# ScalarE issues the loads into buffer A from the first V block on, SyncE those into buffer B

## The chip, the core and the metric

The kernel runs on one core of a Trainium2 chip. The metric is the device time of the program in microseconds (us), the median of several executions. A profiled execution of the same program gives the trace that is quoted below: its times are counted from the first instruction of the span.

Five engines work side by side, each through its own list of instructions: TensorE (PE in the profile, with its weight loads as PEld), VectorE (DVE), ScalarE (ACT), GpSimd (POOL) and SyncE (SP). They wait for each other on semaphores. Loads from the device memory (HBM) are done by 16 DMA engines; a load is issued by an instruction in the list of one of these engines. In the profile, queue q1 holds what SyncE issued and q10 what ScalarE issued.

## What is computed

One decode step of a transformer layer for two sequences: grouped-query attention over a cache of 32768 positions with 32 query heads and 4 KV heads of width 128, in parallel with a SiLU feed-forward block, both on the layer-normed input and both added to it. Everything is float32.

```python
# x: (2, 1, 1024)
xn = layernorm(x)
q = (xn @ wq).reshape(B, 1, 32, 128)                     # wq: (1024, 4096)
k, v = repeat(k_cache, 8), repeat(v_cache, 8)            # caches: (2, 4, 32768, 128)
p = softmax(einsum("bhqd,bhkd->bhqk", q, k) * 128**-0.5)
o = einsum("bhqk,bhkd->bhqd", p, v)
attn = o.reshape(B, 1, 4096) @ wo                        # wo: (4096, 1024)
ffn = silu(xn @ w1) @ w2                                 # w1: (1024, 3584), w2: (3584, 1024)
return x + attn + ffn
```

With one token per sequence nearly all of the data is used once: the caches alone are 268 MB, and 331.4 MB are read in all.

## The kernel before, in words

**Two large buffers.** SBUF holds two buffers, `bufA` and `bufB` (`buf[0]` and `buf[1]`), of 64 KB in each of the 128 partitions, 8.4 MB each. Everything that is read in bulk passes through them in a fixed sequence of 40 steps, alternately A and B: `wq` in two halves, `w1` in two parts, then for each of the 8 pairs of KV head and sequence (`it` in the code) the steps K0 (A), K1 (B), V0 (A), V1 (B), and at the end `wo` in two halves, the first part of `w2` (`w2a`, A, in two pieces) and the second (`w2b`, B, in seven pieces). A full load is one DMA instruction of 128 rows of 64 KB; the 16 DMA engines take 8 rows each.

**TensorE** works through the steps in this order: it waits for the landing of the step's load (`taken`, through `ld`) and for the small operand (`tok`), then runs 64 matmuls of 128x512 over the buffer (`slots`) into PSUM (`xy`), and marks the step as done on `turn_sem`. The buffer is then free.

**VectorE** stands between: with `relay(n)` it waits for the mark of a step and adds one to the semaphore `freed`, on which the loads wait. In `attend()` it relays K0 and K1, then works out the softmax up to the subtraction of the maximum (a transpose, a reduction, two small matmuls on TensorE in between, a subtraction), raises `subbed`, relays V0 and V1, reduces the result, and raises `normed`.

**ScalarE** has a loop of its own over `it`: it waits for `subbed`, does two exponentials that write the weights for V0 and V1 (and raise `tok`), waits for `normed`, and copies the result away (which lets GpSimd stage the weights of the next K0 and K1 through `stage()`).

**SyncE** issues the loads. `load(k, dst, src, s, n)` waits for the event that frees the buffer (`step(n)`: from step 3 on, `freed` has reached n - 2, which means that the step two before, in the same buffer, is done) and issues the DMA. All loads from `w1` to `w2b` stand in SyncE's one list, in the order of the steps. ScalarE issues one DMA, the small `x` (32 KB) at the start.

A step here is named by its block and the value of `it`: K1 of it 0 is the second K block of the first pair.

Of the kernel before, what the change touches and what calls it, by code (L numbers as in the profile page):

```python
# [8 lines left out]
B, HQ, HKV, SK, DH, D, F = 2, 32, 4, 32768, 128, 1024, 3584  # L9
P = 128  # L10
REP = HQ // HKV
W = 16384
# [6 lines left out]
STEPS = 4 + 4 * LOOPS + 4  # L19
# [32 lines left out]
def gqa_plus_mlp_kernel(nc, x8, kt, v0, v1, wq, wo, w1a, w1b, w2a, w2b, out):  # L52
# [4 lines left out]
    sp, T, V, A, G = nc.sync, nc.tensor, nc.vector, nc.scalar, nc.gpsimd  # L57
    sems = [pe.sem, dve.sem, act.sem, pool.sem]

    def sem(name):  # L60
        sems.append(nc.alloc_semaphore(name))
        return sems[-1]

    def sb(name, *shape):
        return nc.alloc_sbuf_tensor(name, shape, F32).ap()
# [4 lines left out]
    buf = [sb(n, P, W) for n in ("bufA", "bufB")]  # L70
    ld, more, tok = ([sem(f"{n}{k}") for k in "AB"] for n in ("ld", "more", "tok"))
# [89 lines left out]
    def step(n):  # L161
        return (turn_sem, n) if n <= 2 else (freed, n - 2)

    def load(k, dst, src, s, n):
        if n:
            sp.wait_ge(*step(n))
        sp.dma_start(buf[k][:, dst] if isinstance(dst, slice) else dst, src).then_inc(s, 16)  # L167

    every = slice(0, W)
    load(0, buf[0].rearrange("p (a n) -> p a n", a=2)[:, :, :6144], w1b, ld[0], 1)  # L170
    load(1, every, w1a, ld[1], 2)
    for it in range(LOOPS):
        h, b = divmod(it, B)
        for j, src in enumerate((kt[b, h, 0], kt[b, h, 1], v0[b, h], v1[b, h])):
            load(j % 2, every, src, ld[j % 2], 3 + 4 * it + j)
    load(0, every, wo[0], ld[0], STEPS - 5)
    load(1, every, wo[1], ld[1], STEPS - 4)
    load(0, slice(0, W // 2), w2a[:, :W // 2], ld[0], STEPS - 3)
    load(0, slice(W // 2, W), w2a[:, W // 2:], more[0], 0)
    cuts = [0, 6 * D, 8 * D, 9 * D, 10 * D, 11 * D, 11 * D + 4 * CUT, 12 * D]  # L180
    for lo, hi, s in zip(cuts, cuts[1:], [ld[1], more[1], *last]):
        load(1, slice(lo, hi), w2b[:, lo:hi], s, STEPS - 2 if lo == 0 else 0)
# [2 lines left out]
    for n in range(4):  # L185
# [6 lines left out]
        a, b = ev[n][:, :512], ev[n][:, 512:]  # L192
# [37 lines left out]
           tqs[:, :, ::16].rearrange("p (h m) b -> p h b m", m=REP)).then_inc(tq, 1)  # L230
    for it in range(LOOPS):
        h, b = divmod(it, B)
        act.wait((subbed, it + 1))
        for c in range(NC):
            A.activation(wt[c].rearrange("p e m -> p (e m)"), st[:, 1024 * c:1024 * c + 1024], AF.Exp,  # L235
                         scale=SCALE).then_inc(tok[c], 1)
        act.wait((normed, it + 1))
        A.copy(oT[:, REP * h:REP * (h + 1), 16 * b], onew).then_inc(tq, 1)  # L238
    for s in (trm, tgd):
        A.sem_inc(s, 1)  # L240
    outs = []
    for n in range(3):
        act.wait(step(STEPS - 3 + n) if n < 2 else (turn_sem, 5))
# [205 lines left out]
```

## Time and profile before

| what | us |
|---|---|
| median of 3 runs | 772.49 (772.41 to 772.53) |
| span of the profiled execution | 771.0 |
| TensorE busy, matmuls | 389.6 |
| VectorE busy | 132.3 |
| GpSimd busy | 44.2 |
| ScalarE busy | 28.4 |

The span is the time from the first to the last instruction of the one profiled execution; the device time of the runs holds a little more, so the median stands 1.5 us above the span. In a row of the timeline the first number is the start, the second the duration, then engine, line, operation and the tiles; what stands in brackets is how long the engine was idle before it, and for whom it waited. "SPq" and "ACTq" are the DMA-issuing instructions of SyncE and ScalarE: the duration there is that of issuing, not of the transfer.

### The profile page before, as it was taken

Reading aid. Unit: us, or ns where it says so; the run is one execution under the profiler, and the core shown is the slowest. Engines: PE = TensorE matmul, PEld = TensorE weight load, DVE = VectorE, ACT = ScalarE, POOL = GpSimd, SP = SyncE. Lnnn points to the kernel's source line nnn. Section 1 sums busy time; section 2 is a strip of 40 time slices with the busy share of each in tenths; the row PEclk is TensorE's granted clock in tenths of the full one; section 3 lists DMA queues with packets and bytes.
Section 4 is the critical chain, followed back from the end, with each engine's and each line's share of the span. In section 5 each row is a group of like instructions: output and inputs, shape, how many; then the busy total and the mean of one; then the engine's idle time right before and its main releaser. Section 6 shows DMA issues by size and latency. Waiting matters only on the chain. (4 is left out here: it accounts for less than half of the span.)

```text
span 771.0 us, 6110 instructions
## 1 busy us (share of the span) xinstructions
PE 389.6 (51%) x2702; PEld 124.5 (16%) x2702; DVE 132.3 (17%) x98; ACT 28.4 (4%) x37; POOL 44.2 (6%) x65
## 2 busy tenths in 40 slices
PE   0454545455545454645455545444645455545466
PEld 0111211121112111211121112111211121112122
DVE  2000104030403040304030303040303030313000
ACT  0000100100010001000100010001000100010000
POOL 3001200000000100010001000100010001000121
PEclk9967677776677777677776677777677776677688
DMA  9999999999999999999999999999999999999997
GB/s 383 435 435 435 435 435 435 435 435 435 435 435 435 435 435 435 435 435 435 435 435 435 435 428 428 418 428 432 425 432 435 435 435 435 435 435 435 435 432 331
DMA packets 6944, 331.40 MB, mean 430 GB/s; under 512 B 776, under 2 KB 920, under 8 KB 1440
## 3 DMA queue, kind: packets, MB, share of 16 engines
q1 hardware_dynamic: 6928, 331.37, 99.5%
q10 hardware_dynamic: 16, 0.03, 0.0%
HBM read 331.38 MB, written 0.02 MB: 430 GB/s over the span
## 5 line engine op out<-in xcount | busy, mean ns | idle before, releaser
L107 PE MATMUL xy<-bufB,weights 128*32 128x512 f32 x1248 | 176.2, 727 | 169.3 <-PEq L49 169.3
L107 PE MATMUL xy<-bufA,weights 128*32 128x512 f32 x1280 | 180.4, 726 | 101.0 <-PEq L49 101.0
L107 PEld LDWEIGHTS xy<-bufB,weights 128*32 128x32 f32 x1248 | 48.8, 131 | 296.7 <-issue 296.5
L107 PEld LDWEIGHTS xy<-bufA,weights 128*32 128x32 f32 x1280 | 49.6, 130 | 215.5 <-issue 215.5
L258 DVE STREAM_TRANSPOSE st<-xy 128x2048 f32<-128x2048 f32 x8 | 18.5, 2316 | 243.2 <-PE xy L107 243.2
L268 DVE TENSOR_REDUCE blank<-xy 128x512 f32<-128x2048 f32 x8 | 18.3, 2292 | 222.8 <-PE xy L107 222.8
L280 POOL MEMSET weights<- 128x2048 f32 x8 | 14.4, 1804 | 525.3 <-POOLq L49 525.3
L107 PE MATMUL smA<-blank 128*8 128x128 f32 x20 | 5.4, 370 | 51.9 <-PEq L49 51.9
L259 DVE TENSOR_REDUCE blank<-st 128x8 f32<-128x2048 f32 x8 | 30.5, 3809 | 0.3
L107 PE MATMUL smA<-blank,ones 128*128 128x8 f32 x18 | 4.9, 347 | 50.6 <-PEq L49 50.6
L269 DVE TENSOR_REDUCE blank<-weights 128x8 f32<-128x2048 f32 x8 | 30.4, 3799 | 0.0
L235 ACT ACTIVATE weights<-st 128x1024 f32<-128x1024 f32 x16 | 16.0, 1048 | 328.3 <-DVE st L265 328.3
L265 DVE TENSOR_TENSOR st<-st,gmax 128x2048 f32<-128x2048 f32 x8 | 18.3, 2293 | 0.3
L107 PE MATMUL smB<-blank 128*128 128x8 f32 x72 | 15.9, 349 | 0.0
L107 PEld LDWEIGHTS smB<-blank 128*128 128x128 f32 x72 | 15.6, 317 | 0.0
L107 PEld LDWEIGHTS smA<-blank,ones 128*128 128x128 f32 x18 | 4.3, 298 | 58.5 <-issue 58.5
L238 ACT COPY blank<-onew 128x8 f32<-128x8 f32 x8 | 1.6, 204 | 277.8 <-DVE onew L272 277.8
L107 PEld LDWEIGHTS smA<-blank 128*8 128x8 f32 x20 | 1.3, 89 | 60.2 <-issue 60.2
L374 DVE TENSOR_TENSOR rest<-ev 128x512 f32<-128x512 f32 x1 | 0.7, 693 | 49.1 <-POOL ev L372 49.1
L107 PE MATMUL smB<-blank,ones 8*128 8x8 f32 x20 | 5.3, 333 | 5.7 <-PEq L49 5.7
L286 POOL COPY weights<-qall 128x128 f32 x32 | 8.0, 292 | 3.1 <-POOL weights L280 3.1
L212 DVE STREAM_TRANSPOSE tqs<-sumq 128x1024 f32<-128x1024 f32 x1 | 1.2, 1245 | 39.4 <-POOL sumq L196 39.4
(54 smaller groups left out, 57.7 us busy)
## 6 DMA issues: line engine op xcount, KB each, us to landing
bufA<-in_w2a SPq DMA_DIRECT2D x2, 4096.0 KB, 23.7
bufA<-in_w1b SPq DMA_DIRECT2D x1, 6144.0 KB, 24.6
bufB<-in_w2b SPq DMA_DIRECT2D x1, 3072.0 KB, 17.9
bufB<-in_w2b SPq DMA_DIRECT2D x3, 512.0 KB, 21.6
bufB<-in_w2b SPq DMA_DIRECT2D x1, 1024.0 KB, 20.0
bufB<-in_w2b SPq DMA_DIRECT2D x1, 384.0 KB, 23.0
bufA<-in_kt SPq DMA_DIRECT2D x8, 27.8
bufB<-in_kt SPq DMA_DIRECT2D x8, 29.2
```

The lines of the kernel that those rows point to most:

```text
L107: return T.matmul(o, lhsT, rhs, start=start, stop=stop)
L212: i_q = dve.mark(V.transpose(tqs.rearrange("p c m -> p (c m)"), sumq))
L235: A.activation(wt[c].rearrange("p e m -> p (e m)"), st[:, 1024 * c:1024 * c + 1024], AF.Exp, scale=SCALE).then_inc(tok[c], 1)
L238: A.copy(oT[:, REP * h:REP * (h + 1), 16 * b], onew).then_inc(tq, 1)
L258: then(3, V.transpose(st, xy))
L259: V.tensor_reduce(rm, e8.rearrange("p n m -> p m n"), AX.X, ALU.max).then_inc(trm, 1)
L265: V.tensor_sub(e8, e8, gmax.to_broadcast([P, 256, REP])).then_inc(subbed, 1)
L268: V.tensor_reduce(ob, xy.rearrange("p (c n) -> p n c", c=4), AX.X, ALU.add).then_inc(tob, 1)
L269: V.tensor_reduce(lsum, weights.rearrange("p e (r m) -> p m (e r)", m=REP), AX.X, ALU.add).then_inc(tls, 1)
L280: G.memset(weights, 0.0).then_inc(pself, 1)
L286: m = G.tensor_copy(o, q[:, None, None, :].to_broadcast([P, 4, 4, REP]))
L374: t = dve.mark(V.tensor_add(rest, ev[0][:, :512], ev[0][:, 512:]))
```

## The change

`load` gets a parameter for the engine that waits and issues. SyncE keeps `wq`, `w1`, the first K0 and everything that goes into buffer B. The later loads into buffer A (all V0, the other K0, the first half of `wo`, both pieces of `w2a`) are issued by ScalarE, each behind the same wait on `freed`. Which bytes are loaded, into which buffer, and on which event each load waits is as before.

```diff
-    def load(k, dst, src, s, n):
+    def load(k, dst, src, s, n, q=sp):
         if n:
-            sp.wait_ge(*step(n))
-        sp.dma_start(buf[k][:, dst] if isinstance(dst, slice) else dst, src).then_inc(s, 16)
+            q.wait_ge(*step(n))
+        q.dma_start(buf[k][:, dst] if isinstance(dst, slice) else dst, src).then_inc(s, 16)
...
     load(1, every, w1a, ld[1], 2)
+    load(0, every, kt[0, 0, 0], ld[0], 3)
     for it in range(LOOPS):
         h, b = divmod(it, B)
-        for j, src in enumerate((kt[b, h, 0], kt[b, h, 1], v0[b, h], v1[b, h])):
-            load(j % 2, every, src, ld[j % 2], 3 + 4 * it + j)
-    load(0, every, wo[0], ld[0], STEPS - 5)
+        for j, src in ((1, kt[b, h, 1]), (3, v1[b, h])):
+            load(1, every, src, ld[1], 3 + 4 * it + j)
     load(1, every, wo[1], ld[1], STEPS - 4)
-    load(0, slice(0, W // 2), w2a[:, :W // 2], ld[0], STEPS - 3)
-    load(0, slice(W // 2, W), w2a[:, W // 2:], more[0], 0)
...
     for it in range(LOOPS):
         h, b = divmod(it, B)
+        load(0, every, v0[b, h], ld[0], 5 + 4 * it, A)
         act.wait((subbed, it + 1))
         for c in range(NC):
             A.activation(wt[c].rearrange("p e m -> p (e m)"), st[:, 1024 * c:1024 * c + 1024], AF.Exp,
                          scale=SCALE).then_inc(tok[c], 1)
+        g, c = divmod(it + 1, B)
+        load(0, every, kt[c, g, 0] if g < HKV else wo[0], ld[0], 7 + 4 * it, A)
         act.wait((normed, it + 1))
         A.copy(oT[:, REP * h:REP * (h + 1), 16 * b], onew).then_inc(tq, 1)
     for s in (trm, tgd):
         A.sem_inc(s, 1)
+    load(0, slice(0, W // 2), w2a[:, :W // 2], ld[0], STEPS - 3, A)
+    load(0, slice(W // 2, W), w2a[:, W // 2:], more[0], 0, A)
```

On SyncE, around the first pair of KV head and sequence, the list of loads changes as follows (a row is the line, the operation, the buffer and the tensor that it is filled from; `in_v` is a V block, `in_kt` a K block; rows with a minus are gone):

```order
 L167 DMA bufA<-in_kt 128x16384
 L167 DMA bufB<-in_kt 128x16384
-L167 DMA bufA<-in_v 128x16384
 L167 DMA bufB<-in_v 128x16384
-L167 DMA bufA<-in_kt 128x16384
 L167 DMA bufB<-in_kt 128x16384
```

Only the loads into buffer B stay, so that a load into B is no longer behind the load into A of the step before it in the list.

On ScalarE, the first turn of the loop over `it` (and the beginning of the second) read before, with what each instruction waits for:

```order
L229 COPY qall<-tqs 128x64 [waits dve]
L235 ACTIVATE weights<-st 128x1024 [waits subbed]
L235 ACTIVATE weights<-st 128x1024
L238 COPY blank<-onew 128x8 [waits normed]
L235 ACTIVATE weights<-st 128x1024 [waits subbed]
```

and read now:

```order
L227 COPY qall<-tqs 128x64 [waits dve]
L167 DMA bufA<-in_v 128x16384 [waits freed]
L234 ACTIVATE weights<-st 128x1024 [waits subbed]
L234 ACTIVATE weights<-st 128x1024
L167 DMA bufA<-in_kt 128x16384 [waits freed]
L239 COPY blank<-onew 128x8 [waits normed]
L167 DMA bufA<-in_v 128x16384 [waits freed]
```

The load of V0 stands ahead of the two exponentials, the load of the next K0 between them and the copy of the result.

## The prediction

> **What bounds the kernel now.** I read the page first, for shares of the span:
>
> ```profile
> span 771.0 us, 6110 instructions
> ...
> PE 389.6 (51%) x2702; PEld 124.5 (16%) x2702; DVE 132.3 (17%) x98; ACT 28.4 (4%) x37; POOL 44.2 (6%) x65
> ...
> q1 hardware_dynamic: 6928, 331.37, 99.5%
> ```
>
> The busiest engine works for half of the span, while SyncE's queue occupies the 16 DMA engines for 99.5% of it. The end is set there as well, as the last rows of the chain that ended last show:
>
> ```profile
> 744.13 21.65 DMA bufB<-in_w2b
> 765.78 0.04 issue
> 765.82 2.95 PE acc L107 x36
> 768.77 0.02 issue
> 768.79 0.37 ACT ot L246
> ```
>
> The time is thus that of moving 331 MB, and the change can only matter by letting the DMA engines run empty, or by what stands behind the last load. Next, the timeline of one turn (SyncE's issues, TensorE's runs over a buffer, the exponentials):
>
> ```profile
> 95.67 8.57 PE L107 MATMUL xy<-bufA,weights 128*32 128x512 f32 x64 [8.43 <-PEq L49]
> ...
> 104.35 0.33 SPq L167 DMA_DIRECT2D bufA<-in_v  x1
> ...
> 115.03 9.13 PE L107 MATMUL xy<-bufB,weights 128*32 128x512 f32 x64 [10.79 <-PEq L49]
> ...
> 124.27 0.33 SPq L167 DMA_DIRECT2D bufB<-in_v  x1
> ...
> 135.06 2.00 ACT L235 ACTIVATE weights<-st 128x1024 f32<-128x1024 f32 x2 [44.91 <-DVE st L265]
> 136.26 8.75 PE L107 MATMUL xy<-bufA,weights 128*32 128x512 f32 x64 [3.77 <-PEq L49]
> ...
> 145.13 0.33 SPq L167 DMA_DIRECT2D bufA<-in_kt  x1
> 153.74 8.54 PE L107 MATMUL xy<-bufB,weights 128*32 128x512 f32 x64 [8.73 <-PEq L49]
> ```
>
> K0 is worked on from 95.67, K1 from 115.03: a load takes 19.36 us of the DMA engines, **2.42 us for each of an engine's 8 rows**. V0's load is issued at 104.35, 0.1 us after the run over K0 ends, when about half of K1 is still to come. In one queue it waits behind K1, and begins when K1 is complete. So a load is always in reserve, by some 8 to 10 us, and the DMA engines never wait for TensorE. That reserve is a property of first come, first served.
>
> **What two queues do.** The question is whether a load in q10 waits for the one in q1, or shares the engines with it. The trace holds one such meeting: ScalarE's small load of x, issued while SyncE's first load runs.
>
> ```profile
> 0.74 0.37 SPq L110 DMA_DIRECT2D bufA<-in_wq  x1
> 1.72 1.13 ACTq L116 DMA_DIRECT2D xs<-in_x  x1
> 10.63 0.33 SPq L118 DMA_DIRECT2D bufB<-in_wq  x1
> 23.00 9.06 PE L107 MATMUL xy<-bufA,weights 128*32 128x512 f32 x64 [23.00 <-PEq L49]
> ...
> out_y<-ot SPq DMA_DIRECT2D x1, 16.0 KB, 1.8
> ```
>
> SyncE's second issue waits for x, and goes out at 10.63: x took 8.9 us. A transfer of similar size on idle engines, the output, takes 1.8. The 7.1 us more are 2.9 rows of 2.42; behind all 8 rows of the first load, x would have come at about 23. So **the queues take turns, row by row**. I read the three rows as two in front of x's data (the one in flight, and the next, already chosen) and one in front of its completion message, which takes its turn like a row.
>
> The same rows give the price of a start from empty: the first load is issued at 0.74 and worked on at 23.00, 22.26 us, of which 19.36 are rows: 2.9 us for issue, start and landing.
>
> The Trainium skill ("DMA: Bandwidth & Descriptors", section "Queues, rings and completion order") states that a DMA engine alternates between queues by packets of typically 9 to 17 descriptors. If a packet held that many of these rows, the 8 rows and the completion of a load would go out in one piece, and nothing would change. By that rule the sum would be nil instead of the one below; the load of x, which passed after about three rows, speaks against it for rows of 64 KB.
>
> **The first turn.** K0 of it 0 is unchanged. V0's load, issued at 104.35, now takes turns with the rest of K1: three of its rows fall before K1's completion, and K1 lands 7.3 us later, at 122.3 in place of 115.03. Its run ends at 131.4. From the end of K1's run (124.16) to the start of V0's (136.26) the softmax takes 12.1 us; so V0 starts at 143.5 and ends at 152.2, and the next K0 is issued at 152.3. V0 and V1 have come without a pause, so V1 is worked on at 153.74 as before. A load back to back with it could be worked on at 153.74 + 19.36 = 173.1; one issued at 152.3 cannot before 152.3 + 22.26 = 174.6. **The DMA engines run empty for 1.5 us.** For the next gap, in which TensorE is not yet fully in the pattern below, I take 2, together 3.5.
>
> **Why it stays so.** Once the engines have run empty, both buffers hold landed data. TensorE works on A, then on B straight after. How long such a run takes depends on what came before:
>
> ```profile
> 174.67 10.02 PE L107 MATMUL xy<-bufA,weights 128*32 128x512 f32 x64 [3.77 <-PEq L49]
> ...
> 743.97 3.64 PE L107 MATMUL xy<-bufA,weights 128*32 128x512 f32 x32 [0.77 <-PEq L49]
> ...
> 753.55 5.58 PE L107 MATMUL xy<-bufA,weights 128*32 128x512 f32 x32 [5.94 <-PEq L49]
> ```
>
> After a gap of 0.77 us 32 matmuls take 3.64, after 5.94 they take 5.58. So A, after a gap, takes 8.5 to 10.0 (8.57, 8.75 and 10.02 above; I take 9.5), and B, straight behind it, 2 x 3.64 = 7.3 at most; I take 7.1. The loads into A and B are therefore issued 7.1 us apart, each time.
>
> A's load then has the engines alone for four rows (three take 7.3 us, the fourth is chosen by then), and the other four take turns with four rows of B; one more row of B comes in front of A's completion: 13 rows. A is worked on 2.9 + 13 x 2.42 = 34.4 us after its issue, done 9.5 later, and its next load is issued 0.1 after that: 44.0 us for a pair. B's remaining three rows need 7.3, less than the 9.5: B has landed before A is free, **the engines are empty again**, and the pattern repeats. A pair needs 2 x 19.36 = 38.7 of the engines, so 5.3 us are lost in each.
>
> In this pattern the softmax, 12.1 us, no longer holds V0 up: V0 lands 34.4 - 7.1 = 27 us after the end of K1's run.
>
> **ScalarE's part.** It issues 18 loads more. On SyncE one takes 0.33, on ScalarE the one of x took 1.13; a longer issue delays A's load by 0 to 0.8 us in each pair, and I take 0.4. Its other work isn't delayed: V0's load waits for K0's end, which is a whole run ahead of the exponentials (they start 10.9 us after K1's run ends), and the next K0's load waits for V0's end, a run and the reductions ahead of the copy. SyncE's issues are not slower, and nothing queues behind a load there that doesn't already wait for a later event.
>
> **The end.** Before, the second piece of w2a lands at 753.5 and w2b is alone after it. Now w2b enters 7.1 us after w2a and takes turns with it: of w2a's 16 rows of 32 KB (1.21 us each) some 6 go alone and 10 with rows of 24 KB of w2b (0.91) between, 28 to 29 us, while both together (8.4 and 6.3 MB) need 33.9. So w2a's last rows come 5 to 6 us before w2b's, and TensorE has its second half (5.58), the 32 matmuls on w2b (3.64) and the last tiles (up to 2.95) still to do: 9.2 to 12.2 less 5 to 6, some 5.5 us more behind the last load than now, when the tiles are worked on as they land.
>
> **The sum.** Gaps in the full pattern stand ahead of the loads K0 and V0 of it 2 to 7, of wo and of w2a: 14. So 14 x (5.3 + 0.4) = 79.8, and 3.5 for the first two, and 5.5 at the end: 88.8 us. The span goes from 771.0 to 859.8; with the 1.5 us between span and median, **861 us**.
>
> Bounds: with runs of 8.5 and a start from empty that costs nothing, a pair takes 31.5 + 8.6 = 40.1, 1.4 lost, 20 in all: 802. If B's first row gets out one row earlier, A needs 14 rows, 2.42 more in each pair, 34 in all: 895. With two streams at once a row might also take longer or less long than 2.42; no row shows it, and 2% either way is 5 us.
>
> **Rivals.**
> - *The reserve survives.* If completion messages don't take a turn, or the queue looks further ahead, K1 lands at 119.9, V0 ends at 149.8 and the next K0 is issued at 149.9. The deciding point is 173.1 - 22.26 = 150.8: earlier than that, the engines stay busy, and no gap opens there. What remains is the end (5.5) and perhaps a gap or two later: 775 to 790, likeliest 779. For it: the margin is one row. Against it: 2.9 rows in front of x.
> - *Whole loads are served in order of arrival* (the other side: not slower). The place is the arbitration between q1 and q10; the price is nothing, since each load is then issued at the same event as before, and begins behind the same one: 772.5. It decides once an engine takes all 9 pieces of a load (8 rows and the completion) in one turn. Against it: x at 10.63 and not at 23. This is what the rule of the Trainium skill named above would give.
> - *Faster.* The queue is at 99.5%, and even the remainder of 0.5% is 4 us; only overlapping starts of rows could win any of it. 770.
>
> **How the numbers follow.** The pattern of gaps, with its bounds: 0.80, range 800 to 900. The surviving reserve: 0.10. Beyond 900: 0.02. Whole loads in order: 0.06. Faster: 0.02. The first holds the 8 in 10 alone, so the range is 800 to 900. Slower by over 0.2% (1.5 us, about what a measurement of this kernel can tell from no change) has 0.92, the same 0.06, faster 0.02.
>
> **What would show it.** In the profile after: q10 with some 140 MB; K1 of it 0 worked on at about 122 (right) or 115 (whole loads in order) or 120 (reserve survives); DMA share by stage at about 0.87 from it 2 on (right), or 0.99 (both rivals); runs over bufB of about 7.1 that start straight behind runs over bufA of 9 to 10, and 34 us from issue to landing for A. The prediction is wrong if the DMA engines show no gap.

## The result and the profile after

The change makes the kernel **slower by 11%**: 856.1 us (median of 6 runs, 852.2 to 860.8) against 772.47 (772.33 to 772.54), a ratio of 1.109 (95% interval 1.107 to 1.111). The profiled execution has a span of 858.0 us, against 771.0. In two of the experiments below one execution came out more than 1.5% above the fastest of its kernel (801.7 us with only V0 on ScalarE, 854.1 with `w2a` on SyncE); it is left out there as slow.

The page after, in the lines that answer to those shown of before:

```profile
span 858.0 us, 6110 instructions
...
PE 368.7 (43%) x2702; PEld 122.7 (14%) x2702; DVE 132.3 (15%) x98; ACT 28.3 (3%) x37; POOL 44.2 (5%) x65
...
q1 hardware_dynamic: 4336, 188.76, 51.0%
q10 hardware_dynamic: 2608, 142.64, 39.7%
```

The bytes and the instructions are the same. But the two queues together occupy the DMA engines for 90.7% of a longer span, where one queue had 99.5%. That is 778 us of 858, against 767 of 771: 76 of the 87 us are time in which the DMA engines have nothing to do. The other 11 are longer work, above all the first row of a load that starts from empty: in the trace's records of the single DMA packets (a packet is a row) the first row of the load issued at 239.85 took 2.51 to 3.49 us on the 16 engines, the others 2.42.

The timeline shows where. First the first turn, and then two of the pairs that follow (TensorE's runs and the issues of both queues, each row with its start and duration):

```profile
95.70 8.69 PE L107 MATMUL xy<-bufA,weights 128*32 128x512 f32 x64 [8.31 <-PEq L49]
104.51 0.35 ACTq L167 DMA_DIRECT2D bufA<-in_v  x1
122.31 9.03 PE L107 MATMUL xy<-bufB,weights 128*32 128x512 f32 x64 [17.93 <-PEq L49]
131.46 0.33 SPq L167 DMA_DIRECT2D bufB<-in_v  x1
...
143.46 8.70 PE L107 MATMUL xy<-bufA,weights 128*32 128x512 f32 x64 [3.76 <-PEq L49]
152.28 0.34 ACTq L167 DMA_DIRECT2D bufA<-in_kt  x1
155.08 7.07 PE L107 MATMUL xy<-bufB,weights 128*32 128x512 f32 x64 [2.92 <-PEq L49]
```

```profile
229.87 9.86 PE L107 MATMUL xy<-bufA,weights 128*32 128x512 f32 x64 [19.38 <-PEq L49]
239.54 7.05 PE L107 MATMUL xy<-bufB,weights 128*32 128x512 f32 x64
239.85 0.33 ACTq L167 DMA_DIRECT2D bufA<-in_kt  x1
246.71 0.33 SPq L167 DMA_DIRECT2D bufB<-in_kt  x1
...
274.05 9.96 PE L107 MATMUL xy<-bufA,weights 128*32 128x512 f32 x64 [18.85 <-PEq L49]
283.82 7.05 PE L107 MATMUL xy<-bufB,weights 128*32 128x512 f32 x64
284.13 0.33 ACTq L167 DMA_DIRECT2D bufA<-in_v  x1
```

In the first turn K1 is worked on at 122.31 where it was 115.03 before. In the pairs, A's load is issued at 239.85, B's 6.9 us later, A is worked on 34.2 us after its issue, TensorE runs over A for 10.0 and over B for 7.05 straight behind it, and A is issued again at 284.13. Cut at these moments, the table of stages gives the state of the DMA engines (start and end, length, busy time of PE, PEld, DVE, ACT, POOL, granted clock, DMA share, GB/s):

```profile
239.85:274.05 34.20, 9.02 (x74) 4.10 (x67) 6.38 (x4) 0.20 (x1) 2.80 (x5) 0.64 1.01 429
274.05:284.13 10.08, 10.08 (x68) 2.88 (x72) 0.00 (x0) 0.00 (x0) 0.00 (x0) 0.71 0.48 208
280.70:285.05 4.35, 4.35 (x44) 1.33 (x40) 0.00 (x0) 0.00 (x0) 0.00 (x0) 1.00 0.00 0
```

While loads are under way, the engines move 430 GB/s, as much as before with one queue. While TensorE runs over A, they finish B's last rows, by 280.7 in the packet records (the table counts a row at its start, so the 0.48 leaves out a part of them). The last row of the table is what follows: until A's next load begins at 285.1 no row is under way on any engine, 4.4 us.

The order of the rows is on record too. Between A's issue and its landing, from 240.5 to 272.8, the DMA view counts these packets and megabytes in the two queues:

```profile
q10 hardware_dynamic: 128, 8.39, 62.2%
q1 hardware_dynamic: 80, 5.24, 37.4%
```

On each of the 16 engines these are eight rows of A and five of B: four of A alone, then one of B and one of A in turn, then a fifth of B, and only behind it A's completion message. Three rows of B are left.

### The profile page after: what moved, and what is told of

It reads as the page before. It is cut to its first block, busy times and chain, and to the rows that moved or that the text cites. A ratio compares the mean times of both kernels' runs of the same rounds, so it can differ in the third digit from the quotient of the medians.

```text
span 858.0 us, 6110 instructions
## 1 busy us (share of the span) xinstructions
PE 368.7 (43%) x2702; PEld 122.7 (14%) x2702; DVE 132.3 (15%) x98; ACT 28.3 (3%) x37; POOL 44.2 (5%) x65
## 5 line engine op out<-in xcount | busy, mean ns | idle before, releaser
L107 PE MATMUL xy<-bufA,weights 128*32 128x512 f32 x1280 | 194.0, 773 | 336.8 <-PEq L49 336.8
L107 PE MATMUL xy<-bufB,weights 128*32 128x512 f32 x1248 | 145.1, 618 | 41.1 <-PEq L49 41.1
L107 PEld LDWEIGHTS xy<-bufA,weights 128*32 128x32 f32 x1280 | 52.5, 137 | 461.9 <-issue 461.9
L107 PEld LDWEIGHTS xy<-bufB,weights 128*32 128x32 f32 x1248 | 43.6, 114 | 139.7 <-issue 139.7
## 6 DMA issues: line engine op xcount, KB each, us to landing
bufA<-in_w2a ACTq DMA_DIRECT2D x2, 4096.0 KB, 21.7
bufB<-in_kt SPq DMA_DIRECT2D x8, 34.3
```

The lines of the kernel that those rows point to most:

```text
L107: return T.matmul(o, lhsT, rhs, start=start, stop=stop)
```

## The experiments

The theory: the DMA engines take turns between two queues, a row at a time, so a load that is issued early as a reserve delays the load that is due. Rivals: ScalarE's issues are dear; two queues slow the transfers as such; TensorE (its time or its clock) sets the pace. Each edit is against the change, if not said otherwise.

### Which engine issues

**All loads from V0 of it 0 on by ScalarE**, in the old order:

```diff
...
         load(0, every, v0[b, h], ld[0], 5 + 4 * it, A)
+        load(1, every, v1[b, h], ld[1], 6 + 4 * it, A)
...
         load(0, every, kt[c, g, 0] if g < HKV else wo[0], ld[0], 7 + 4 * it, A)
+        load(1, every, kt[c, g, 1] if g < HKV else wo[1], ld[1], 8 + 4 * it, A)
...
```

> ScalarE issues every load from V0 of it 0 on, those into buffer A and those into buffer B, in the old order; SyncE only the first six and the output. Theory (two queues take turns row by row, so the load in reserve slows the one that is due, and the engines run empty): with one queue nothing is shared, 771 to 774 us, DMA share 0.99, K1 of it 0 worked on at 115. Rival (what ScalarE issues is slower, 84 us for 18 loads, 4.7 each): with about 40 loads on ScalarE well over 900, or at the least as slow as the change, 850.

Measured: 774.7 us, ratio 1.003 (1.002 to 1.004), a little above the 771 to 774 that I expected. ScalarE issues more than twice as many loads as in the change, and nearly the whole loss is gone. One detail was expected wrongly: K1 of it 0 was worked on at 122.4 and not at 115, because it was still SyncE's, and met ScalarE's V0 at the hand-over. Are the 2.2 us left that one meeting, or a price of ScalarE's issues? Two runs tell it apart.

**All loads from the first on by ScalarE**; x goes to SyncE:

```diff
-    sp.dma_start(buf[0], wq[0]).then_inc(ld[0], 16)
+    A.dma_start(buf[0], wq[0]).then_inc(ld[0], 16)
...
     for n in range(4):
+        load(n % 2, *((buf[0].rearrange("p (a n) -> p a n", a=2)[:, :, :6144], w1b), (every, w1a),
+                      (every, kt[0, 0, 0]), (every, kt[0, 0, 1]))[n], ld[n % 2], n + 1, A)
         act.wait(step(n + 1))
...
```

> Every load from the first on is issued by ScalarE in the old order; SyncE issues only x at the start and the output. No load of one queue is ever under way beside a load of the other. Theory: the 2.2 us by which the run with all loads from V0 of it 0 on ScalarE was slower come from the one meeting at the hand-over (K1 of it 0 in SyncE's queue, V0 in ScalarE's); without it the time is that of before, 772.5 (772 to 773.5). Rival (ScalarE's 40 issues have a small price of their own, 0.05 us each): 774.5 again.

Measured: 772.8 us, ratio 1.0005 (0.9996 to 1.0014). Without a meeting of two large loads there is no loss; ScalarE's issues are free here.

**Only V0 of it 0 by ScalarE**, all others by SyncE as before (diff against the kernel before):

```diff
...
+        if it == 0:
+            load(0, every, v0[b, h], ld[0], 5 + 4 * it, A)
```

> One load alone, V0 of it 0, is issued by ScalarE, everything else by SyncE as before. Theory: it meets K1 of it 0, which is worked on at 122.3; one gap of 1.5 to 2.5 us opens before K0 of it 1, then the single queue builds the reserve up again: 774 to 775. Eight such meetings, at 2.2 to 2.5 each, are then the 20 us of the run in which only the V0 loads are on ScalarE. Rival (what that run lost comes from loads that fall further and further behind): 772.5 to 773, and the loss per meeting grows with their number.

Measured: 774.6 us, ratio 1.003 (1.002 to 1.004). One meeting costs 2.1 us, and then it is over. Its timeline:

```profile
122.37 9.19 PE L107 MATMUL xy<-bufB,weights 128*32 128x512 f32 x64 [17.76 <-PEq L49]
131.68 0.33 SPq L167 DMA_DIRECT2D bufB<-in_v  x1
...
143.68 8.78 PE L107 MATMUL xy<-bufA,weights 128*32 128x512 f32 x64 [3.76 <-PEq L49]
152.57 0.33 SPq L167 DMA_DIRECT2D bufA<-in_kt  x1
155.12 7.08 PE L107 MATMUL xy<-bufB,weights 128*32 128x512 f32 x64 [2.66 <-PEq L49]
```

K1, V0 and the issue of K0 fall as in the change. V1 is worked on at 155.1, 1.4 us later than before (153.74), although it is issued while V0's last rows are still under way. The packet records show where: one of the 16 engines begins V1 only at 134.30, though all have finished V0 by 133.7, and ends it at 154.50, where the others end it by 153.5.

**Only the 8 loads of V0 by ScalarE**; K0, wo and w2a by SyncE in their old place:

```diff
...
         load(0, every, v0[b, h], ld[0], 5 + 4 * it, A)
...
-        load(0, every, kt[c, g, 0] if g < HKV else wo[0], ld[0], 7 + 4 * it, A)
...
```

> Only the 8 loads of V0 go to ScalarE; K0, wo and w2a are back with SyncE in their old place. Theory: in each turn V0 meets K1 once and makes it 7.3 us late, then three loads in a row go through one queue and the reserve is built up again; so one gap of 1 to 3 us in each turn and no lasting pattern: 778 us (774 to 784). Rival (a price for each load of ScalarE, 4.7 us): 772.5 + 8 x 4.7 = 810. Rival (two queues in use slow the transfers as such): half of the loss, about 815.

Measured: 790.3 us (median of three runs, 788.8 to 795.3), ratio 1.025 (1.021 to 1.029): less than either rival, more than I expected. Eight times the 2.1 us of the single meeting is 17 of these 17.8 us, so the meetings explain the loss within the scatter. My 778 made a meeting cost 0.7, a third of that; it did not even follow from my own gap of 1 to 3 us in each turn, which makes 8 to 24 us.

**The buffers exchanged**: ScalarE issues B from V1 of it 0 on, SyncE all of A:

```diff
...
-        load(0, every, v0[b, h], ld[0], 5 + 4 * it, A)
+        load(1, every, v1[b, h], ld[1], 6 + 4 * it, A)
...
-        load(0, every, kt[c, g, 0] if g < HKV else wo[0], ld[0], 7 + 4 * it, A)
+        load(1, every, kt[c, g, 1] if g < HKV else wo[1], ld[1], 8 + 4 * it, A)
...
```

> Buffers exchanged between the queues: ScalarE issues the loads into buffer B from V1 of it 0 on, SyncE all into buffer A. Theory: which engine issues does not matter, the pattern is the same: 850 to 866, runs over A of 9 to 10 us after a gap, runs over B of 7.05 straight behind, 34 us from issue to landing on A. Rival (ScalarE's loads are the slow ones): the 34 us move to B, and B is waited for.

Measured in a single execution: 857.5 us. The pattern is the same with the engines exchanged: SyncE issues K0 at 678.41, ScalarE's K1 follows 6.9 us later, and A is worked on 34.3 us after its issue:

```profile
668.31 9.98 PE L107 MATMUL xy<-bufA,weights 128*32 128x512 f32 x64 [19.17 <-PEq L49]
678.11 7.05 PE L107 MATMUL xy<-bufB,weights 128*32 128x512 f32 x64
712.67 9.99 PE L107 MATMUL xy<-bufA,weights 128*32 128x512 f32 x64 [18.90 <-PEq L49]
```

### Turns by row, or shares by bytes

**Rows of 16 KB in buffer A**, those of B left at 64 KB. Each load of a K or V block or of `wo` into A becomes two DMAs of 128 x 2 rows, alternate quarters of a partition (the first half of `wq`, the part of `w1` and `w2a` that go into A get rows of 16 to 32 KB):

```diff
...
+        if k == 0 and src.shape == (P, W):
+            dst, src = (t.rearrange("p (a b n) -> p b a n", a=2, b=2) for t in (dst, src))
+            parts = [(dst[:, i], src[:, i]) for i in range(2)]
...
-        pe.take(ld[k], 16)
+        pe.take(ld[k], 32 if k == 0 else 16)
```

> The change, but each load into buffer A is cut into rows of 16 KB (two DMAs of 128 x 2 rows), B's stay at 64 KB. Theory (the queues take turns row by row, whatever a row holds): beside a load of B, A gets a fifth of the engines and B four fifths. K1 of it 0 is delayed less and is worked on at 117 instead of 122.3; from then on A's load, which is the one that is due, crawls behind B's: B lands long before A, and the engines are empty for 12 us in each pair. 976 us (940 to 1000). Rival (the queues share by bytes, or the loss is that of two queues as such): 850 to 870, K1 at 122.

> The kernel before (one queue, SyncE) with the same rows of 16 KB in buffer A, to take out what the rows cost by themselves. Theory: nothing, 771 to 774 us. If smaller rows are slower by themselves: the same part of what the run with two queues shows.

Measured: 976.5 us with two queues, ratio 1.264 (1.260 to 1.268); 776.7 with one queue, ratio 1.005 (1.003 to 1.008). The smaller rows cost 4.2 us by themselves, where I had expected nothing, and 120 us more in the change. K1 of it 0 is worked on at 117.01. A pair, in the timeline and in the table of stages:

```profile
407.77 9.13 PE L107 MATMUL xy<-bufA,weights 128*32 128x512 f32 x64 [26.60 <-PEq L49]
416.71 7.06 PE L107 MATMUL xy<-bufB,weights 128*32 128x512 f32 x64
417.02 1.21 ACTq L177 DMA_DIRECT2D bufA<-in_v  x2
423.88 0.33 SPq L177 DMA_DIRECT2D bufB<-in_v  x1
...
458.91 9.16 PE L107 MATMUL xy<-bufA,weights 128*32 128x512 f32 x64 [26.80 <-PEq L49]
```

```profile
417.00:459.00 42.00, 8.00 (x72) 2.65 (x68) 9.08 (x6) 2.00 (x2) 0.00 (x0) 0.64 0.94 399
459.00:470.00 11.00, 11.00 (x84) 3.20 (x88) 0.00 (x0) 0.00 (x0) 0.00 (x0) 0.81 0.09 19
```

A is worked on 41.9 us after its issue in place of 34.2, and while TensorE runs over it there is nothing left to load: the DMA share is 0.09. B, issued later, passed A with its larger rows. The packet records show the turns one by one: from 429 to 450.45 there are 112 rows of each queue, one of A (0.61 us) between any two of B (2.42 us). With shares by bytes the size of a row would not matter.

### What makes the pattern last

**Half of the matmuls left out, in the runs over A or in those over B** (32 of 64; `0` or `1` for the buffer). The output lacks them; the loads are the same.

```diff
-            for r in range(4):
+            for r in ((0, 3) if k == 0 else range(4)):
```

> The change, with half of the matmuls left out of each run over buffer A (32 of 64), so the output lacks them. Theory: A's run of 10 us is what the load in B cannot outlast; with 5 to 6.5 us A is issued again before B has landed, the reserve survives for most of the time and the loss goes nearly all: 777 us (774 to 800). Rival (the transfers are slower with two queues): 850 or more.

> The change, with half of the matmuls left out of each run over buffer B. Theory: less work, but slower: B is then issued 3.6 to 5 us after A instead of 7.1, so A has the engines alone for one row less, 14 rows before its landing instead of 13, 2.4 us more in each pair: 880 us (872 to 892). Rival (TensorE's time or clock sets the pair): faster than the change, by the same as with half of the runs over A.

Measured, in two executions each: with the shorter runs over A 778.3 us (1.004 to 1.010 times before), with the shorter runs over B **898.1** (1.159 to 1.166), more than the 872 to 892 that I expected. The same work is left out in both, and one loses nearly all of the loss, the other adds 42 us. This settles that TensorE's time is not the price itself: what counts is when the runs let the two loads start. With half runs over A:

```profile
412.13 6.26 PE L107 MATMUL xy<-bufA,weights 128*32 128x512 f32 x32 [4.52 <-PEq L49]
418.51 0.33 ACTq L167 DMA_DIRECT2D bufA<-in_v  x1
431.48 8.56 PE L107 MATMUL xy<-bufB,weights 128*32 128x512 f32 x64 [13.09 <-PEq L49]
440.16 0.33 SPq L167 DMA_DIRECT2D bufB<-in_v  x1
```

A is issued 13 us before B's load has even landed; the two issues lie 21.7 us apart. With half runs over B:

```profile
432.57 3.62 PE L107 MATMUL xy<-bufB,weights 128*32 128x512 f32 x32
432.88 0.33 ACTq L167 DMA_DIRECT2D bufA<-in_kt  x1
436.30 0.33 SPq L167 DMA_DIRECT2D bufB<-in_kt  x1
471.81 9.33 PE L107 MATMUL xy<-bufA,weights 128*32 128x512 f32 x64 [27.02 <-PEq L49]
```

The issues lie 3.4 us apart and A is worked on 38.9 us after its own. With 2.9 us for the start that leaves 36.0, or 15 rows of 2.42, where the change has 13 and I expected 14. This pair is one of the longer ones: by the packet records 15 of the 16 engines go through 14 rows in it, three of A alone and then in turn, and report A landed by 469.3. On one engine a row of B (at 439.77) comes ahead of the third row of A, and the load waits for that engine until 471.5. In the next pair A is issued at 481.26 and worked on at 517.93, 36.7 us later, which is 14 rows. From the issue of K0 of it 2 (246.29) to that of `w2a` (850.47) 13 pairs take 46.5 us each, 2.4 more than in the change: the one row that was expected. They make 31 of the 40 us between the two profiled spans (897.9 and 858.0); another 6.4 are lost ahead of them and 2.6 behind, which I had not reckoned with.

### The end

**w2a by SyncE**, ahead of w2b as before; the rest of the change stays:

```diff
+    load(0, slice(0, W // 2), w2a[:, :W // 2], ld[0], STEPS - 3)
+    load(0, slice(W // 2, W), w2a[:, W // 2:], more[0], 0)
...
-    load(0, slice(0, W // 2), w2a[:, :W // 2], ld[0], STEPS - 3, A)
-    load(0, slice(W // 2, W), w2a[:, W // 2:], more[0], 0, A)
```

> The change, but with both pieces of w2a issued by SyncE, ahead of w2b as before. Theory: the gaps stay, w2a no longer takes turns with w2b and lands about 14 us before the end instead of 7, so that only the last tiles are left behind the last load: 5 us less than the change (851 where the change gives 856), and 2 to 3 us from the last landing to the end instead of 8. If the end was not mis-ordered by the sharing: the same as the change.

Measured: 848.7 us (median of three runs, 840.6 to 850.5), 7.4 us less than the change; each of the three lies below the lowest of the change, 852.2. The chain that ended last, in the change, shows what had to be done behind the last landing of `w2a` (rows of less than 0.1 us left out):

```profile
843.08 5.36 PE xy L107 x32
...
848.47 1.02 ACT ev L247
...
849.62 2.39 POOL ev L375
...
852.04 0.70 DVE rest L377
...
852.77 0.70 DVE blank L379
...
853.51 2.18 PE acc L107 x28
```

The second half of w2a, its copy and the sums that need it stand in a row there, with no DMA among them. From the issue of w2a (813.17) to the end of the span are 44.8 us; with SyncE issuing w2a (798.42) 40.8, since its second half is worked on at 820.27, 19 us before the end in place of 15. Those 4.0 us are the end by itself, from one execution of each; the other 3.4 of the medians lie within what both versions scatter.

## Why the prediction was right

- **Turns between the queues.** Right, and the centre of it: K1 of it 0 at 122.31 (122.3 predicted), V0 at 143.46 (143.5), the next K0 issued at 152.28 (152.3). The packet records and the runs with rows of 16 KB show that the turn is by row. The load of x was read rightly as well: in the records of before its rows start at 7.03, behind two rows of the first load (from 1.74 and 4.62), and its completion at 9.65, behind one more.
- **Why it stays so.** Right: runs of 10 and 7.05 us straight behind each other, loads 6.9 us apart, 34.2 us from the issue of A's load to the run over it (34.4 predicted from 13 rows, and 13 are on record). The DMA share by stage is 0.89 to 0.91 from 233 us on (0.87 predicted). The runs with half of the matmuls show that the lengths of A's and of B's run work in opposite directions, as the pattern needs.
- **The price of a pair.** From the issue of K0 of it 2 (239.85) to that of w2a (813.17) are 573.3 us for 13 pairs, 44.1 each, so 5.4 lost in each, in place of 5.7: 14 x 5.4 = 75.6 for a predicted 79.8. Two errors met in it: ScalarE's issue takes 0.33 us and not the 1.13 that the load of x suggested, so the 0.4 for it was wrong; and the runs over A mostly take 9.7 to 10.0 us, not 9.5.
- **The first two gaps.** Too small: K0 of it 2 is worked on at 274.05. One queue without a pause would have had it at 153.74 + 5 x 19.36 = 250.5, and five rows of B that precede it in its turns are 12.1 more, 262.6. Of the 11.5 us lost by then 5.4 belong to K0's own pair, so the first two cost 6.1 in place of 3.5. The step that failed is "V0 and V1 have come without a pause": V1 comes 1.3 us late (1.4 with the single meeting alone), because one of the 16 engines begins and ends it about a microsecond after the others. K0 of it 1, behind four rows of B, could have been worked on at 173.1 + 9.7 = 182.8 and is at 185.32: the first gap cost 2.5 in place of 1.5. The other 3.6 belong to the second, for which 2 was a guess.
- **The end.** 87.0 - 75.6 - 6.1 leaves 5.3 (5.5 predicted); measured by itself 4.0.
- **The total.** It came closer than its parts, by luck: 4.2 us too much for the pairs and 2.6 too little for the first gaps make a span of 859.8 for a measured 858.0. That execution is one of the longer ones; the median, 856.1, lies 5 us under the 861 predicted.
- **The rivals.** That whole loads are served in order of arrival falls with K1 at 122.3. That the reserve survives is not what this kernel does, but what it does with shorter runs over A: 778.3, in the range that was given for it.

The scatter has grown as well, 852 to 861 us in place of 0.2: the length of a run over A, 8.4 to 10.0 in the trace, now goes into every pair, where one queue hid it. That this is the cause is likely and not shown; the granted clock of TensorE was 0.684 in the longest of the six runs and 0.697 in the shortest.

## What to carry to other kernels

Two queues don't add bandwidth to DMA engines that one queue keeps busy, and they take away the order: in one queue a load issued early is a reserve, in a second queue it is a competitor of the load that is due. Keep loads that are needed one after the other in one queue, whichever engine issues it, and before moving any, look for the load that is in flight when the moved one is issued. Where a pipeline has two buffers, ask whether both can be full at once: from then on nothing is in flight, and less work on one engine can make the kernel slower.

## What was not expected of the hardware

- The size of a row decides the share: beside rows of 64 KB, a load with rows of 16 KB took 41.9 us from its issue to the run over it, one with rows of 64 KB 34.2.
- The completion message of a load takes its turn like a row: A's came at 272.84 to 273.42 on the 16 engines, behind a fifth row of B, though A's own last row had ended by 271.0.
- ScalarE issued a load of 128 rows in 0.33 us, as SyncE does; the load of x (8 rows) took it 1.13.
- V1, issued 2 us before the other queue's load was complete, still came 1.3 to 1.4 us later than without a pause. One of the 16 engines began it 0.6 to 0.9 us after the last row of V0 had ended (134.30 against 133.69, 134.49 against 133.62); why wasn't tried.
